# The planner's durations corrected, and two small steps given a choice of engine

## The chip, the cores and the metric

The kernel runs on one core of one Trainium2 chip. Five engines work side by side, each through its own instruction queue in order: PE (TensorE, matrix products), DVE (VectorE), ACT (ScalarE), POOL (GpSimd) and SP (SyncE, which issues the DMA transfers here). They meet through semaphores. The metric is the device time of one execution in microseconds.

## The reference

Attention with decay for 8 batches of 8 heads, 576 positions and 64 columns a head, and behind it a feed-forward layer with the Mish gate on 4608 rows:

```
scores = scale * np.matmul(q, k.transpose(0, 1, 3, 2))
cum = np.cumsum(np.log(np.clip(f, 0.0001, 1.0)), axis=-1)
decay = cum[:, :, :, None] - cum[:, :, None, :]
scores = np.where(causal, -1000000000.0, scores + decay)
attn = np.exp(scores - np.max(scores, axis=-1, keepdims=True))
attn = attn / (np.sum(attn, axis=-1, keepdims=True) + 1e-09)
x = np.matmul(attn, v)          # heads side by side: 4608 x 512
h = x @ w_in                    # 512 x 2048
sp = np.where(h > 20.0, h, np.log1p(np.exp(np.minimum(h, 20.0))))
out = (h * np.tanh(sp)) @ w_out # 2048 x 512
```

## The kernel before

**The work.** Heads go in pairs: 4 pairs a batch, 32 pairs in all. For the first 6 pairs the row maxima are found in a pass of their own (`max_items`): scores on PE, maxima on DVE (tiles `mx`, `m`), a transpose on PE and a copy of the turned maxima into the tile `mr`, from where DMAs put them beside the scores' operands. The other 26 pairs find maxima and exponentials in one pass (`new_st_items`; DVE writes `mn`, ACT the exponentials into `st`), split them in two halves of 16 bits (`hb`) and turn them by DMA (`pt`). The products with the values stand in a PSUM bank as four or five blocks of 128 rows by 65 columns; the 65th column is the row's sum. DVE turns the sums into factors (`rr`), and the division is the product of each block with its factor, from the bank into the tile `x`. `x` is split in two halves (`xp`) and turned by DMA into `xa`, the feed-forward layer's operand. That layer works in 9 chunks of 512 rows (8 of the batches, the ninth of what the batches leave over) and 16 steps of 128 hidden columns: products of `xa` with the weights `wall`, Mish on ACT (`me`), two halves for the next product (`gh`, `gl` on DVE, some `gh` on ACT), and products of those with the second weights. Products of the layer are 3456 of 512 columns.

**Tables on ACT.** Mish and the exponential lie in different function tables, so ACT loads a table each time that it goes from one to the other.

**Banks.** Of PSUM's eight banks four hold the layer's sums, two its hidden values; after the opening all of attention shares the two that are left.

**Order.** Nothing of the order is written by hand. Class `Program` records every operation, its reads and writes, and runs a model of the five queues (`schedule`): forward, always taking the ripe operation with the lowest rank, then backward to get ranks from the end, ten forward passes in all; the order of the best forward pass is issued. `choose` records an operation that may run in several ways, each on one engine, and the forward pass takes the way that ends sooner in the model. `cost` gives the model's duration of one operation. Two constants, `TSWAP` and 1370 ns, are the model's price for a table. In the opening, until the first product with `wall`, the forward pass also puts in products of the identity with itself where the model has PE idle: filler products, 128x128, which nobody reads (line 307 of before, 311 of the changed kernel). All other operations are issued from one line (310 of before, 314 of the changed kernel), so tiles tell them apart in the profile, not lines.

**Lines the change touches.** The division in `one` of `pv_items` and `new_pv_items` is one DVE instruction over all blocks; in `new_pv_items` the fifth block is one `tensor_scalar` more. The copy into `mr` in `fin` is a DVE copy. In `cost` a `tensor_scalar` between buffers in SBUF is reckoned at 1.92 elements a ns, whatever the strides, and only `scalar_tensor_tensor` is charged 60 ns for a scalar that comes from memory.

Of the kernel before, what the change touches and what calls it, by code (L numbers as in the profile page):

```python
# [13 lines left out]
F16 = mybir.dt.float16  # L14
# [6 lines left out]
AF = mybir.ActivationFunctionType  # L21
ALU = mybir.AluOpType
# [4 lines left out]
P = 128  # L27
S = 576
D = 64
# [119 lines left out]
class Program:  # L149
# [24 lines left out]
    def choose(self, *ways):  # L174

        r, w, opts = [], [], []
        for way in ways:
            total, port = 0.0, False
            for nth, (eng, method, a, kw) in enumerate(way):
                aps = [(k, x) for k, x in list(enumerate(a)) + list(kw.items()) if hasattr(x, "tensor")]  # L180
                w += [z for k, x in aps if k in ("out", "accum_out", 0) for z in self.region(x)]
                r += [z for k, x in aps if k not in ("out", "accum_out", 0) for z in self.region(x)]
                if eng == "scalar":
                    (r if method == "activation" else w).append(("table", 0, 1, 0, 1))
                if eng == "tensor":

                    out = kw["out"] if "out" in kw else a[0]
                    w.append((out.tensor.name + "/pe", 0, 1, 0, 1))
                port |= self.shared(eng, method, aps)
                cost = self.cost(eng, method, kw, aps)  # L190
                if isinstance(cost, tuple) and total:

                    total = (
                        total[0] + (53 if nth == 1 else 8 if nth % 2 else cost[0]), total[1] + cost[1], 0, cost[3])
                else:
                    total = cost if isinstance(cost, tuple) else total + cost + (80 if total else 0)
            opts.append((eng, way, total, port))
        key = len(self.ops)
        if self.rank is not None:
            key, self.rank[1] = self.rank[0] + self.rank[1], self.rank[1] + self.rank[2]  # L200
        self.ops.append((opts, r, w, key))
        self.floors.append(self.floor)
        func = ways[0][0][3].get("func") if ways[0][0][0] == "scalar" and len(ways) == 1 else None
        self.sets.append("mish" if func == AF.Mish else "exp" if func == AF.Exp else None)

        self.banks.append({
            x.tensor.name for _, _, a, kw in ways[0] for x in list(a) + list(kw.values())
            if hasattr(x, "tensor") and x.space == PSUM})
# [26 lines left out]
    def cost(self, eng, method, kw, aps):  # L235

        out = next((x for k, x in aps if k in ("out", 0)), None)
        srcs = [x for k, x in aps if k in ("in_", "in0", "in1", "data0")]
        n = max([free(x) for x in srcs[:1]] + [1]) if method == "tensor_reduce" else free(out) if out is not None else 1
        psum = any(x.space == PSUM for x in srcs)  # L240
        if method.startswith("dma_start"):
            size = free(out) * int(out.shape[0]) * mybir.dt.size(out.dtype)
            if method == "dma_start_transpose":
                return 1190 + size / 3000.0 + DH, size / 292.0
            return (450 if DRAM in (kw["in_"].space, out.space) else 625) + DH, size / DRATE
        if eng == "tensor":

            rows = int(kw.get("in_", kw.get("rhs")).shape[0])
            half = (int(out.offset) // int(out.ap[0][0]) // 64 + 1) * (int(out.shape[0]) == 64)
            part = rows * (free(kw["lhsT"]) if "lhsT" in kw else int(out.shape[0])) / 128.0**2  # L250
            if kw.get("rhs") is not None and kw["rhs"].dtype == F32:
                part *= 4 * n
                n = max(4 * n, 4 * int(out.shape[0]) + 22)
            else:
                part *= n
            return max(n, 64), part, half, int(out.shape[0]) == 64
        if eng == "scalar":
            if method != "activation":
                return 1283
            t = (51 if psum else 93) + n / 1.2  # L260
            t += 93 * any(k in ("scale", "bias") for k, x in aps) + 93 * ("accum_out" in kw)
            return t
        if eng == "vector":
            if method == "reciprocal":
                return 68 + 6 * n
            fast = method in ("tensor_scalar", "tensor_copy") and not psum
            if method == "tensor_tensor_reduce":
                return 76 + n / 0.96 + 60 * hasattr(kw["scalar"], "tensor")
            return 68 + n / (1.92 if fast else 0.96) + 60 * (method == "scalar_tensor_tensor" and "scalar" in dict(aps))
        if method == "tensor_tensor":  # L270
            b = kw["in1"]
            return 148 + (1.88 if mybir.dt.size(b.dtype) == 2 and int(b.ap[-1][0]) == 1 else 2.1) * n
        if method == "tensor_scalar":
            return 247 + 0.83 * n
        if method == "affine_select":
            return 136 + 0.85 * n
        return 43 + 0.82 * n
# [97 lines left out]
    def forward(self, deps, succ, rank):  # L375
        ops = self.ops
        n = len(ops)
# [11 lines left out]
        table = "exp"  # L389

        left, half, mode, recent = {}, 0, False, []

        def arrive(i):
            for o, (q, _, _, _) in enumerate(ops[i][0]):
# [24 lines left out]
        while len(order) < n + fills:  # L419
            clock["sync"] = max(clock["sync"], hw, dma - BACK)  # L420
            best = None
            for q in self.NAMES:
# [5 lines left out]
                if r or c:  # L428
                    t = clock[q] if r else max(clock[q], c[0][0])
                    if best is None or (t, q) < best:  # L430
                        best = (t, q)
            t, q = best
            while coming[q] and coming[q][0][0] <= t:
                _, i, o = heappop(coming[q])
# [59 lines left out]
            else:  # L494
                if q == "tensor":
                    filling = filling and ops[i][0][o][1][0][3].get("lhsT", self.idle[1]).tensor.name != self.last
                    e, full = clock[q], t - IDLE
                    while recent and recent[0][0] < t - TICK:
                        recent.pop(0)
                    dense = sum(w for _, w in recent)  # L500
                    while filling and began and e < full and dense < NEED:
                        k = int((e + 197.0) / TICK)
                        warm = left.get(int(e / TICK) - 1, 0.0) >= WARM
                        e += P / (2.4 if warm else 1.2) + 2.5
                        left[k] = left.get(k, 0.0) + P
                        recent.append((e, P))
                        dense += P * (e >= t - TICK)
                        order.insert(-1, (-1, 0))
                        fills += 1
                    began = True  # L510
                    t = max(t, e)
                    cols, weight, h, m = cost
                    if m != mode:
                        t += 97.0
                    mode = m
                    slow = 1.0 if left.get(int(t / TICK) - 1, 0.0) >= WARM else 2.0
                    cost = 22.0 if h and half and h != half else cols * slow / 2.4 + (2.5 if slow < 2 else 0.0)
                    a, b = (t + 197.0) / TICK, (t + 197.0 + cols * slow / 2.4) / TICK
                    for k in range(int(a), int(b) + 1):
                        left[k] = left.get(k, 0.0) + weight * (min(b, k + 1) - max(a, k)) / (b - a)  # L520
                    half = h
                    recent.append((t + cols * slow / 2.4, weight))
                elif lock:
                    port = max(t, port) + cost
                    cost = port - t
                elif q == "scalar" and self.sets[i] not in (None, table):
                    table = self.sets[i]
                    cost += 1370.0
                clock[q] = t + cost
# [70 lines left out]
def attn_moe(ctx: ExitStack, tc: tile.TileContext, qk, v, f, w_in, w_out, out):  # L600
# [423 lines left out]
    def max_items(g):  # L1024
# [63 lines left out]
        def fin():  # L1088
# [5 lines left out]
            ps = bank(f"mtp{g}", (P, P), F16)  # L1094
            nc.tensor.transpose(out=ps[0:9, :], in_=m16, identity=idh)
            mr = sp.tile([9, P], F16, name=f"mr{g}", tag="mr", bufs=2)
            nc.vector.tensor_copy(out=mr, in_=ps[0:9, :])
            for j in range(2):
                nc.sync.dma_start(
                    out=q1[MROW : MROW + 1, j, 0:CH].rearrange("o (t c) -> o t c", c=P),  # L1100
# [184 lines left out]
    def new_pv_items(g):  # L1285
# [29 lines left out]
        def one(j):  # L1315
# [17 lines left out]
            nc.vector.reciprocal(out=rr, in_=rr)  # L1333
            if j == 0:
                s["x"] = sp.tile([P, 10, D], F32, name=f"x{g}", tag="x32", bufs=NX)
            nc.vector.tensor_tensor(
                out=s["x"][:, j:8:2], in0=o[:, 0:4, 0:D],
                in1=rr[:, 0:4].unsqueeze(2).to_broadcast([P, 4, D]), op=ALU.mult)
            if j:
                nc.vector.tensor_scalar(  # L1340
                    out=s["x"][:, 8:10], in0=o[:, 4:5, 0:D].to_broadcast([P, 2, D]),
# [4 lines left out]
    def pv_items(g):  # L1346
# [30 lines left out]
        def one(j):  # L1377
# [5 lines left out]
            nc.vector.reciprocal(out=rr, in_=rr)  # L1383
            if j == 0:
                s["x"] = sp.tile([P, 10, D], F32, name=f"x{g}", tag="x32", bufs=NX)
            nc.vector.tensor_tensor(
                out=s["x"][:, j::2], in0=o[:, :, 0:D],
                in1=rr.unsqueeze(2).to_broadcast([P, 5, D]), op=ALU.mult)

        return [(lambda: one(0), 45 * 30), (lambda: one(1), 40 * 30)]  # L1390

# [335 lines left out]
```

## Time and profile before

| | |
|---|---|
| median of 3 runs | 1024.47 us (1024.3 to 1038.92) |
| the profiled execution, its own time | 1024.42 us |
| its span, first to last instruction | 1022.6 us |
| instructions | 19788 |
| PE busy | 986.9 us |
| DVE busy | 698.1 us |
| ACT busy | 690.9 us |

Outside the span lie 1.8 us. Busy times are sums over the span; consecutive instructions of one engine overlap a little in the records, and a PE that is busy is not PE at its peak.

### The profile page before, as it was taken

To read this page: it belongs to the slowest core of one execution; us is meant where nothing else is said; L and a number is where in the kernel's file an instruction comes from. 1 tells how busy PE (TensorE), PEld (TensorE's weight loads), DVE (VectorE), ACT (ScalarE), POOL (GpSimd) and SP (SyncE) were. 2 spreads that over 40 slices of the span, in tenths; PEclk is the share of its full clock that TensorE was granted. 3 is DMA by queue.
4 is the path that set the end of the run, shared out by engine and by line. 5 is a ranking of instruction groups with operands and counts; after the bars stand their busy time and mean duration, and the time that the engine had idled before them with its cause. 6 is when DMAs were issued, how large, how long until landed. Compare 5 with 4: busy or idle time off the path is not lost.

```text
span 1022.6 us, 19788 instructions
## 1 busy us (share of the span) xinstructions
PE 986.9 (97%) x7296; PEld 524.1 (51%) x7296; DVE 698.1 (68%) x1960; ACT 690.9 (68%) x1236; POOL 9.3 (1%) x56
## 2 busy tenths in 40 slices
PE   4999999989999999999999999999999999999998
PEld 3886564444554555554445555554555554444443
DVE  8999999977877877787777877787776562121211
ACT  6766989868778877787777786787777763212112
POOL 1000000000000000000000000000000000000000
PEclk9999999999999999999999999999999999999999
DMA  7889577987776876678777677767666431001001
GB/s 233 277 227 280 193 189 164 225 188 165 152 151 152 189 156 136 143 174 154 139 138 176 144 165 138 159 135 132 117 138 108 78 68 55 1 1 42 1 0 42
DMA packets 251644, 141.25 MB, mean 138 GB/s; under 512 B 220172, under 2 KB 220556, under 8 KB 251546
## 3 DMA queue, kind: packets, MB, share of 16 engines
q1 hardware_dynamic: 251546, 139.98, 60.4%
q8 instruction: 57, 0.93, 0.4%
q14 instruction: 41, 0.34, 0.1%
HBM read 47.76 MB, written 11.76 MB: 58 GB/s over the span
## 4 chain that ended last, share of the span: by engine, by line
PE 67%; DVE 10%; ACT 9%; DMA 7%; issue 3%; SPq 1%; ACTq 0%; DVEq 0%
PE b L310 66%; DMA st<-hl 3%; DMA qk<-in_qk_dram 2%; ACT L310 2%; ACT st L310 2%; DVE wall L310 2%; DVE hl L310 2%; DMA pt<-hb 2%; DVE b L310 1%; ACT junk L310 1%; DVE hb L310 1%; ACT me L310 1%; ACT hb L310 1%; SPq L310 1%; DVE gl L310 1%
## 5 line engine op out<-in xcount | busy, mean ns | idle before, releaser
L310 PEld LDWEIGHTS <-wall 128*128 128x128 f16 x3456 | 330.2, 98 | 373.4 <-issue 4.3
L310 PE MATMUL b<-xa,wall 128*128 128x512 f16 x1728 | 402.9, 379 | 2.8 <-ACT me L310 2.5
L310 PE MATMUL b<-gh,wall 128*128 128x512 f16 x1152 | 360.0, 379 | 0.6 <-DVE ot L310 0.6
L310 PE MATMUL b<-gl,wall 128*128 128x512 f16 x576 | 218.3, 379 | 0.0
L310 ACT ACTIVATE me<-b,cinv 128x512 f32<-128x512 f32 x144 | 93.0, 684 | 123.3 <-PE b L310 122.7
L310 ACT ACTIVATE st<-b,mn 128x512 f32<-128x512 f32 (+2 forms) x260 | 125.0, 523 | 66.6 <-DVE mn L310 50.5
L310 PE MATMUL b<-st 70*128 70x128 f16 (+15 forms) x948 | 142.2, 288 | 23.4 <-DVE qt L310 13.7
L310 DVE TENSOR_TENSOR hb<-st,hb 128x512 f16<-128x512 f32 x156 | 107.2, 688 | 67.8 <-ACT hb L310 67.1
L310 DVE TENSOR_SCALAR gh<-me,gsc 128x512 f16<-128x512 f32 x117 | 54.3, 481 | 140.1 <-ACT me L310 139.0
L310 ACT ACT_TABLE_LOAD x110 | 141.1, 1283 | 1.9
L310 PE MATMUL b<-vv,pt 128*128 128x65 f16 (+5 forms) x2520 | 116.8, 204 | 4.4 <-DMA pt<-hb 2.2
L310 PEld LDWEIGHTS <-st 70*128 70x128 f16 (+4 forms) x948 | 72.5, 103 | 80.3 <-issue 27.5
L310 DVE CUSTOM_DVE_ANT_0 b<-b,mskw 128x512 f32<-128x512 f32 (+1 forms) x208 | 102.2, 497 | 16.6 <-PE b L310 10.8
L310 ACT ACTIVATE hb<-st 128x512 f16<-128x512 f32 x156 | 97.2, 629 | 20.0 <-DMA pt<-hb 19.0
L310 DVE SCALAR_TENSOR_TENSOR gl<-me,gsc,gh 128x512 f16<-128x512 f32 x144 | 102.3, 746 | 0.6
L310 PEld LDWEIGHTS <-pt 128*128 128x128 f16 (+1 forms) x2184 | 70.0, 101 | 25.3 <-DMA pt<-hb 4.9
L310 DVE SCALAR_TENSOR_TENSOR hl<-qk,qt,hl 128x576 f16<-128x576 f32 x64 | 50.9, 811 | 3.3 <-ACT hl L310 3.1
L310 ACT ACTIVATE junk<-qk 128x576 bf16<-128x576 f32 x64 | 43.6, 682 | 9.8 <-DMA qk<-in_qk_dram 8.9
L310 DVE SCALAR_TENSOR_TENSOR wall<-wall 128x512 int32<-128x512 int32 x64 | 42.8, 676 | 0.1
L310 PEld LDWEIGHTS b<-vv,pt 128*128 128x128 f32 (+1 forms) x336 | 38.4, 184 | 3.5 <-issue 1.0
L310 ACT ACTIVATE ot<-b,cols 128x512 f32<-128x512 f32 x36 | 23.9, 684 | 21.5 <-PE b L310 12.1
L310 ACT ACTIVATE vv<-v,cols 128x576 f16<-128x576 f32 (+1 forms) x21 | 16.2, 772 | 31.5 <-PE b L310 31.5
(107 smaller groups left out, 646.1 us busy)
## 6 DMA issues: line engine op xcount, KB each, us to landing
st<-hl SPq DMA_DIRECT2D x186, 144.0 KB
qk<-in_qk_dram SPq DMA_DIRECT2D x32, 576.0 KB
v<-in_v_dram SPq DMA_DIRECT2D x32, 288.0 KB
out_dram<-ot SPq DMA_DIRECT2D x36, 256.0 KB
wall<-in_w_in_dram SPq DMA_DIRECT2D x16, 512.0 KB
wall<-in_w_out_dram SPq DMA_DIRECT2D x16, 512.0 KB
pt<-hb SPq DMA_TRANSPOSE x156
part<-ot SPq DMA_DIRECT2D x8, 256.0 KB
```

Source lines behind the costliest of these rows:

```text
L310: r = getattr(real[eng], method)(*a, **kw)
```

## The change

Three things. The division and the copy into `mr` may now run on DVE or on ACT, as the model chooses; on ACT the division is one ACTIVATE for each block of 64 columns, with the factor as its scale. `cost` charges 60 ns for any scalar from memory (`gh`, `hl`, the fifth block's `x`), takes the fast rate only where the input's and output's strides make one run (the copy of values into `vv` has gaps of one column), and 110 ns more for ACT's copies to 64 partitions of 16 bits. The forward pass charges 175 ns (DVE) or 126 ns (ACT) for a reduction right behind another one, and 8 ns instead of 80 between the parts of a way on ACT.

```
-                    total = cost if isinstance(cost, tuple) else total + cost + (80 if total else 0)
+                    total = cost if isinstance(cost, tuple) else total + cost + ((8 if eng == "scalar" else 80) if total else 0)
...
+            if int(out.shape[0]) == 64 and kw["in_"].dtype == F16:
+                t += 110
...
-            fast = method in ("tensor_scalar", "tensor_copy") and not psum
+            dims = [(int(s), int(m)) for s, m in list(out.ap)[1:] if m > 1]
+            whole = all(a == b * m for (a, _), (b, m) in zip(dims, dims[1:]))
+            fast = method in ("tensor_scalar", "tensor_copy") and not psum and whole
...
-            return 68 + n / (1.92 if fast else 0.96) + 60 * (method == "scalar_tensor_tensor" and "scalar" in dict(aps))
+            return 68 + n / (1.92 if fast else 0.96) + 60 * ("scalar" in dict(aps) or "scalar1" in dict(aps))
...
+        summed = dict(vector=[175.0, False], scalar=[126.0, False])
...
-                elif q == "scalar" and self.sets[i] not in (None, table):
+                if q in summed:
+                    sums = "accum_out" in way[0][3]
+                    cost += summed[q][0] * (sums and summed[q][1])
+                    summed[q][1] = sums
+                if q == "scalar" and self.sets[i] not in (None, table):
...
-            nc.vector.tensor_copy(out=mr, in_=ps[0:9, :])
+            nc.choose(*(scaled(mr, ps[0:9, :], None, e) for e in ("vector", "scalar")))
...
-            nc.vector.tensor_tensor(
-                out=s["x"][:, j::2], in0=o[:, :, 0:D],
-                in1=rr.unsqueeze(2).to_broadcast([P, 5, D]), op=ALU.mult)
+            nc.choose(
+                [("vector", "tensor_tensor", (), dict(
+                    out=s["x"][:, j::2], in0=o[:, :, 0:D],
+                    in1=rr.unsqueeze(2).to_broadcast([P, 5, D]), op=ALU.mult))],
+                [("scalar", "activation", (), dict(
+                        out=s["x"][:, 2 * t + j], in_=o[:, t, 0:D], func=AF.Copy, scale=rr[:, t : t + 1]))
+                    for t in range(5)])
```

The other division, in `new_pv_items`, is changed alike with four blocks. Since ranks and choices all hang on the model, every engine's order is another one. Counted over the built programs: of 64 divisions 24 go to ACT (5 of the first twelve, which have five blocks, and 19 of four blocks, 101 ACTIVATEs in all), and all 6 copies into `mr`. From DVE to ACT go also 8 of the 32 copies into `vv`, 6 of the 64 into `hl` and 3 of the 144 into `gh`; from ACT to DVE 15 of the 32 wide copies into `xp` and 2 of the 32 into `wall`. ACT loads 112 tables in place of 110 and PE has 178 filler products in place of 120. All other instructions are the same in number and engine.

Three places. First the DVE queue in the opening, where the first pair is divided, of before. Names are a tile's, with its buffer's number; `b_0_...` are PSUM banks.

```order
L310 TENSOR_SCALAR rr_146<-b_0_122 128x5
L310 TENSOR_SCALAR wsq<-wsq 128x6
L310 SCALAR_TENSOR_TENSOR wall<-wall 128x512
L310 RECIPROCAL rr_146<-rr_146 128x5
L310 TENSOR_REDUCE mx_144<-b_0_123 128x4
L310 TENSOR_TENSOR x_0_147<-b_0_122,rr_146 128x5x64
```

The same place of the DVE queue now:

```order
L314 TENSOR_SCALAR rr_146<-b_0_122 128x5
L314 TENSOR_SCALAR wall<-wall 128x512
L314 RECIPROCAL rr_146<-rr_146 128x5
L314 TENSOR_REDUCE mx_144<-b_0_123 128x4
L314 SCALAR_TENSOR_TENSOR wall<-wall 128x512 x3
L314 TENSOR_SCALAR wall<-wall 128x512
L314 SCALAR_TENSOR_TENSOR wall<-wall 128x512
```

And the ACT queue at that place now:

```order
L314 ACTIVATE mr_138<-b_0_125 9x128
L314 ACTIVATE junk_107,wsq<-wall 128x512
L314 ACTIVATE x_0_147<-b_0_122,rr_146 128x64 x5
L314 ACTIVATE junk_107,vc_155<-v_4_142 128x576
L314 ACTIVATE junk_107,vc_155<-v_5_143 128x576
L314 ACTIVATE junk_107,wsq<-wall 128x512
```

The division of the first half left DVE for ACT as five instructions, and DVE fills the place with the conversion of weights.

Second the PE queue some fifty rows in, between the maxima of the first pair (`st_0`) and of the second (`st_1`), of before:

```order
L310 MATMUL b_0_125<-st_0_81 64x64
L310 LDWEIGHTS idm
L310 MATMUL b_0_125<-msk_77,idm 128x64
L310 LDWEIGHTS st_1_82
L310 MATMUL b_0_121<-st_1_82 128x128
```

And now:

```order
L314 MATMUL b_0_125<-st_0_81 64x64
L314 LDWEIGHTS idm
L314 MATMUL b_0_125<-msk_77,idm 128x64
L311 LDWEIGHTS idh
L311 MATMUL b_0_105<-idh 128x128
L311 LDWEIGHTS idh
L311 MATMUL b_0_105<-idh 128x128
L311 LDWEIGHTS idh
L311 MATMUL b_0_105<-idh 128x128
L311 LDWEIGHTS idh
L311 MATMUL b_0_105<-idh 128x128
L314 LDWEIGHTS st_1_82
```

Four filler products came in ahead of the second pair; 54 more are spread over the rest of the opening. Ahead of the first product with `wall` stand 505 other products in before and 518 now.

Third the ACT queue in the middle of the program, where one pair has its exponentials between two loads for Mish, of before:

```order
L310 ACT_TABLE_LOAD
L310 ACTIVATE st_2_83<-b_0_125,mn_178 128x512
L310 ACTIVATE hb_181<-st_2_83 128x512
L310 ACTIVATE hl_111<-qk_0_103,qt_108 128x576
L310 ACTIVATE st_2_83<-b_0_119,mn_178 128x512
L310 ACTIVATE hb_182<-st_2_83 128x512
L310 ACTIVATE st_2_83<-b_0_125,mn_178 128x128
```

And now:

```order
L314 ACT_TABLE_LOAD
L314 ACTIVATE st_2_83<-b_0_125,mn_178 128x512
L314 ACTIVATE hb_181<-st_2_83 128x512
L314 ACTIVATE hl_111<-qk_0_103,qt_108 128x576 x2
L314 ACTIVATE vv_141<-v_1_113,cols 128x9x64
L314 ACTIVATE st_2_83<-b_0_119,mn_178 128x512
L314 ACTIVATE x_0_147<-b_0_125,rr_159 128x64 x4
L314 ACTIVATE st_2_83<-b_0_125,mn_178 128x128
L314 ACTIVATE hb_182<-st_2_83 128x512
```

Between the exponentials of one pair ACT now also has a copy of values, one `hl` more and the division of an earlier pair.

## Rows read from the trace of the kernel before

**Rows 1.** The page: busy us of the span, and tenths by slice.

```profile
PE 986.9 (97%) x7296; PEld 524.1 (51%) x7296; DVE 698.1 (68%) x1960; ACT 690.9 (68%) x1236; POOL 9.3 (1%) x56
...
PE   4999999989999999999999999999999999999998
...
PEclk9999999999999999999999999999999999999999
```

**Rows 2.** Busy us of each engine in four stretches; POOL, clock, DMA behind.

```profile
0.00:100.00 100.00, 83.63 (x800) 66.30 (x801) 92.42 (x258) 68.07 (x143) 5.51 (x29) 1.00 0.87 252
100.00:250.00 150.00, 142.28 (x1001) 76.39 (x1000) 134.33 (x403) 128.65 (x247) 0.84 (x6) 1.00 0.77 192
250.00:845.00 595.00, 587.87 (x4698) 303.11 (x4697) 439.90 (x1252) 453.13 (x785) 2.90 (x21) 1.00 0.69 141
845.00:1022.60 177.60, 173.10 (x802) 78.27 (x800) 31.44 (x50) 41.09 (x63) 0.00 (x0) 1.00 0.06 20
```

**Rows 3.** What PE waited for: us in total, times, longest.

```profile
PE b L310 <- DVE qt L310: 13.7, 1, 13.7
PE b L310 <- ACT st L310: 5.8, 8, 1.2
PE b L310 <- ACT me L310: 2.5, 2, 1.4
...
PE b L310 <- DVE x L310: 1.7, 2, 1.3
```

**Rows 4.** Groups of DVE by form: busy us, mean ns, then idle before.

```profile
L310 DVE TENSOR_SCALAR gh<-me,gsc 128x512 f16<-128x512 f32 x117 | 54.3, 481 | 140.1 <-ACT me L310 139.0
...
L310 DVE SCALAR_TENSOR_TENSOR wall<-wall 128x512 int32<-128x512 int32 x64 | 42.8, 676 | 0.1
...
L310 DVE TENSOR_TENSOR x<-b,rr 128x256 f32<-128x256 f32 x52 | 21.9, 421 | 3.7 <-ACT st L310 3.3
...
L310 DVE TENSOR_SCALAR hl<-qk,qt 128x576 f16<-128x576 f32 x34 | 17.4, 517 | 15.2 <-DMA st<-hl 14.7
...
L310 DVE TENSOR_SCALAR vv<-v,cols 128x576 f16<-128x576 f32 x10 | 8.0, 803 | 0.0
...
L310 DVE TENSOR_TENSOR x<-b,rr 128x320 f32<-128x320 f32 x12 | 5.8, 481 | 0.0
...
L310 DVE CAST xp<-x 128x512 f16<-128x512 f32 x7 | 2.9, 418 | 0.0
...
L310 DVE COPY mr<-b 9x128 f16<-9x128 f16 x6 | 1.2, 208 | 0.2 <-PE b L310 0.2
```

**Rows 5.** Groups of ACT by form: busy us, mean ns, then idle before.

```profile
L310 ACT ACT_TABLE_LOAD x110 | 141.1, 1283 | 1.9
...
L310 ACT ACTIVATE pt<-b 128x512 f32<-128x512 f32 x36 | 20.0, 592 | 3.8 <-PE b L310 3.6
...
L310 ACT ACTIVATE xp<-x 128x512 f16<-128x512 f32 x25 | 15.6, 624 | 4.4 <-DVE x L310 4.4
L310 ACT ACTIVATE vv<-v,cols 128x576 f16<-128x576 f32 x16 | 12.4, 772 | 29.5 <-PE b L310 29.5
...
L310 ACT ACTIVATE e<-b 128x64 f32<-128x64 f32 x6 | 1.3, 222 | 4.6 <-PE b L310 4.5
```

**Rows 6.** Timeline of ACT at 288 us: start, us, what.

```profile
288.01 0.35 ACT L310 ACTIVATE st<-b,mn 128x128 f32<-128x128 f32 x1
288.37 1.28 ACT L310 ACT_TABLE_LOAD   x1
289.67 1.26 ACT L310 ACTIVATE me<-b,cinv 128x512 f32<-128x512 f32 x2
```

**Rows 7.** Timeline of PE: filler products at either clock, start, us, what.

```profile
19.52 1.70 PE L307 MATMUL b<-idh 128*128 128x128 f16 x14
...
83.01 2.40 PE L307 MATMUL b<-idh 128*128 128x128 f16 x40
```

**Rows 8.** Products with `wall`: duration ns min/median/max, first and last start us.

```profile
L310 PE MATMUL b<-xa,wall x1728: 376/379/390, 90.6 to 1007.4; 128*128 128x512 f16 x192
```

More of the change, by code (lines that the diff above doesn't have):

```diff
@@ L1335, in one @@
                 s["x"] = sp.tile([P, 10, D], F32, name=f"x{g}", tag="x32", bufs=NX)
-            nc.vector.tensor_tensor(
-                out=s["x"][:, j:8:2], in0=o[:, 0:4, 0:D],
-                in1=rr[:, 0:4].unsqueeze(2).to_broadcast([P, 4, D]), op=ALU.mult)
+            nc.choose(
+                [("vector", "tensor_tensor", (), dict(
+                    out=s["x"][:, j:8:2], in0=o[:, 0:4, 0:D],
+                    in1=rr[:, 0:4].unsqueeze(2).to_broadcast([P, 4, D]), op=ALU.mult))],
+                [("scalar", "activation", (), dict(
+                        out=s["x"][:, 2 * t + j], in_=o[:, t, 0:D], func=AF.Copy, scale=rr[:, t : t + 1]))
+                    for t in range(4)])
             if j:
@@ L1385, in one @@
                 s["x"] = sp.tile([P, 10, D], F32, name=f"x{g}", tag="x32", bufs=NX)
-            nc.vector.tensor_tensor(
-                out=s["x"][:, j::2], in0=o[:, :, 0:D],
-                in1=rr.unsqueeze(2).to_broadcast([P, 5, D]), op=ALU.mult)
+            nc.choose(
+                [("vector", "tensor_tensor", (), dict(
+                    out=s["x"][:, j::2], in0=o[:, :, 0:D],
+                    in1=rr.unsqueeze(2).to_broadcast([P, 5, D]), op=ALU.mult))],
+                [("scalar", "activation", (), dict(
+                        out=s["x"][:, 2 * t + j], in_=o[:, t, 0:D], func=AF.Copy, scale=rr[:, t : t + 1]))
+                    for t in range(5)])
         return [(lambda: one(0), 45 * 30), (lambda: one(1), 40 * 30)]
```

## The prediction

> **What bounds the kernel now.** Start with the page's busy times and slices [rows 1]: PE is busy for 986.9 of 1022.6 us, near nine tenths in every slice but the first, at a granted clock near full throughout, while DVE and ACT stand at 68%. So the question is not how fast DVE or ACT are, but how much time PE loses, and where. The split in four stretches answers the second half [rows 2]. In the first 100 us PE loses 16.4, from 100 to 250 us 7.7, from 250 to 845 us 7.1, and from 845 us to the end 4.5: 35.7 in all. The last stretch holds the feed-forward layer alone (DVE 31 and ACT 41 of 178 us), and its loss is the drain of the last outputs. PE's own waits say the same from the other side [rows 3]: the longest is the first, 13.7 us until the first operands are ready, and the longest after it is 1.3 us. What the change can touch is therefore 35.7 - 13.7 - 4.5 = 17.5 us of idle time, in many small pieces. To that come filler products in the opening, 120 of them; they are busy time that does no work.
>
> One step further: where is an engine other than PE near its limit? From 100 to 250 us DVE is busy 134.3 of 150 and ACT 128.7, because weights are still converted there beside attention; in the opening DVE has 92.4 of 100 [rows 2]. After 250 us they fall to 74% and 76%. So DVE's and ACT's work is worth time before 250 us; behind that only the order is.
>
> **What leaves DVE and what comes to ACT.** DVE loses 19 x 0.421 + 5 x 0.481 = 10.4 us of division, 6 x 0.208 = 1.2 of `mr`, 8 x 0.803 = 6.4 of `vv`, 6 x 0.517 = 3.1 of `hl` and 3 x 0.481 = 1.4 of `gh`; it gains 15 x 0.418 = 6.3 of `xp` and, by `gh`'s row, 2 x 0.481 = 1.0 of `wall` [rows 4]. Sum: 15 us less, 683 for 698.
>
> The division on ACT is not in the trace, an ACTIVATE of 64 columns from PSUM with a scale from memory. The nearest row is the one without that scale, `e`, 0.222 us [rows 5]. A scale from memory adds 0.1: the pair of `me` (512 columns from PSUM, with such a scale) takes 1.26 us, and one of `pt` (the same without) 0.592, so a pair of `me` without overlap would be above 1.18 [rows 5, 6]. Bounds for one: 0.2 if consecutive ones overlap as that pair does by about a tenth, 0.32 if not. I take 0.21, since they stand back to back: 101 x 0.21 = 21 us (32 at the other end). The copy of `mr` costs 6 x about 0.27, by `e`'s row and its 64 columns more: 1.6. Then 17 copies of `vv`, `hl` and `gh` at up to 0.772 are 13, 17 fewer of `xp` and `wall` by `xp`'s row, 0.624, are 10.6, and two more tables 2 x 1.283 = 2.6 [rows 5]. Sum: 27 us more (38 at most), 718 for 691. Neither engine reaches PE's load; on the whole this costs nothing, hidden behind PE's products.
>
> On the tables: in the trace a load is followed by the next ACTIVATE at once (288.37 + 1.28, next start 289.67), and the ACTIVATE ahead ends where the load starts [rows 6], so I price a switch at its load. The Trainium skill ("ScalarE: Activation LUTs", What ACT_TABLE_LOAD costs) adds about 1380 ns of drain to the 1283 ns of a load; the load agrees with the row, the drain is not to be seen in it, and by the page the two tables would cost 5.3 us on ACT in place of 2.6.
>
> **The opening.** The first product with `wall` starts at 90.6 us [rows 8]; it needs the fourth pair's `x`, split and turned. I counted what stands on DVE ahead of the fourth pair's split: 223 instructions before, 225 now. Four divisions, five `mr` and two scalings of weights are gone (1.9 + 1.0 and, at `wall`'s 0.676 each, 1.4 us); but 5 conversions of `wall` (5 x 0.676 = 3.4), 3 `hl` (1.6), an `xp` (0.4) came in, and four maxima and two shorter steps of conversion, taken at half of 0.676 each (2.0) [rows 4]. Net 3 us more ahead of that point. The conversions are not new, only earlier: up to the 17th `gl` DVE has 2.5 us less to do than before, ACT up to the 17th `me` 6 us more. PE's opening grows by 3 us less the thirteen products that now come ahead of `wall`, about 1 us. The 58 further fillers are priced from both ends. If they lie in waits that PE has anyway, they cost nothing; the four ahead of the second pair do, where PE now waits for maxima. If all push, they cost 58 x 0.06 = 3.5 us at the spacing of 83 us (40 in 2.40) or 58 x 0.12 = 7 at that of 19.5 us (14 in 1.70), which is half the pace [rows 7]. I take nothing: the model puts them where it sees PE idle, and DVE's 3 us make such a place. Opening: +2 us (0 to +7; not under 0, since DVE's queue there is longer).
>
> **100 to 250 us.** DVE, the fuller engine, is 2.5 us ahead of before at the 17th `gl`, having been 3 behind at the start; ACT is 6 behind and has 21 us of air in this stretch [rows 2]. Half of DVE's gain on PE's 7.7 us of idle seems fair, and the truer durations help most where engines are full: -2 us (-6 to +5, where +5 is ACT's 6 us more, if it becomes the late one).
>
> **250 to 845 us.** The old table was short by 60 ns for each of 117 `gh`, 34 `hl` and 26 of the fifth block's `x`, and for `vv` reckoned 0.37 us where the row has 0.803: in all some 14 us that DVE was later than planned [rows 4]. PE's order follows the plan, so a truer plan makes it ask less often for what is not there. But PE idles for 7.1 us only, and what it names is mostly ACT's `st`, 5.8 over the whole run [rows 2, 3], the engine that now gets more. -2 us (-6 to +8: everything gone, or the moved divisions felt).
>
> **The sum.** Against the profiled execution's 1024.4 us: +2 - 2 - 2 gives 1022.4, and the median of the runs is the same within 0.1. I predict 1022 us. Two per cent, about what a measurement of this kernel can tell from no change, is 1004 to 1045.
>
> **Rivals.** *The truer plan takes nearly all waits away.* PE's waits between start and drain fall from 17.5 to about 5, and the opening doesn't grow: 1024.4 - 12 = 1012. For it: PE's waits are short and many, as a misjudged order makes them. Against: the opening's queue is longer by count, and a constant such as `TSWAP` was left as it stood. Even all 17.5 us give 1007, so a gain of over 2% needs a shorter opening on top.
>
> *The divisions on ACT hold PE up.* A division frees its PSUM bank. On DVE it took 0.42 to 0.48 us, on ACT four or five times 0.21 and one more semaphore from `rr`, so 0.5 to 0.7 us longer; and it stands in a queue where two tables and a pair of Mish, 1.28 x 2 + 1.26 = 3.8 us, can be ahead of it [rows 5, 6]. Attention has two banks; PE's next scores wait for one. If each of the 24 divisions is felt by its own length, that is 24 x 0.6 = 14 us, and with a third of the queue ahead 24 x 1.2 more, so 1037 to 1066. I put it at 1037 to 1045. It decides if PE's waits name `x` on ACT for over 10 us. For it: ACT's waits of `st` already head PE's list. Against: the plan charges these holds, and PE has products with `wall` to put between. The Trainium skill ("ScalarE: Activation LUTs", Rules for kernel authors) speaks on this side: it gives multiplications to VectorE and not to ScalarE. By length alone the row of DVE, 0.421 for all blocks, agrees with it; what the page leaves open is which engine has time.
>
> *The order is just another draw.* Nothing systematic comes of it, the small waits fall elsewhere: 1024 +- 5. This isn't told apart from the forecast by the time alone.
>
> **How the numbers follow.** Forecast with the last rival, 1015 to 1031: 0.64. Nearly all waits gone, 1007 to 1015: 0.16, of it under 1004 no more than 0.02. ACT holds PE up, 1031 and more: 0.20, of it over 1045 0.07. The range of 8 in 10 takes the forecast's whole, most of the first rival and half of the second: 1010 to 1036. The terms' ends, -12 and +20, would reach 1012 to 1044; all three late at once is unlikely. Chances: 0.02 faster, 0.91 within 2%, 0.07 slower.
>
> **What the profile after would show.** PE still near 987 us busy plus up to 4 of fillers; the first product with `wall` at 92 to 94 us; DVE near 683 and ACT near 718; an ACTIVATE of `x` of 0.3 us in the records, four in about 0.95; attention's end still near 845 us, and the last stretch as before. PE's waits from 100 to 845 us should fall from 14.8 to about 11. I am wrong if the opening lengthens by much more than DVE's 3 us (then the fillers push, or `mr` on ACT comes late), or if PE waits for ACT's `x`.

## The result and the profile after

The changed kernel takes 1013.82 us (median), the kernel before 1024.24 in the same runs: a ratio of 0.9909, 95% interval 0.9896 to 0.9922. That is 10 us less, against a forecast of 2 less. Some executions of any of these kernels run their opening at a lower granted clock and are longer for it; the comparison leaves the most disturbed ones out, and where it matters below a time stands with its execution's mean granted clock.

The page of the changed kernel, to be read against [rows 1]:

```profile
span 1011.2 us, 19990 instructions
...
PE 985.7 (97%) x7354; PEld 526.0 (52%) x7354; DVE 688.0 (68%) x1930; ACT 713.9 (71%) x1345; POOL 9.3 (1%) x56
```

PE's busy time is what it was, within 1.2 us, with 58 filler products more in it. DVE has 10 us less and ACT 23 more. Nearly the whole gain is idle time of PE: 25.5 us in place of 35.7, 10.2 of the 11.4 us by which the span is shorter. The four stretches of [rows 2], of the changed kernel:

```profile
0.00:100.00 100.00, 84.03 (x866) 69.07 (x867) 91.94 (x264) 73.16 (x176) 5.51 (x29) 1.00 0.89 247
100.00:250.00 150.00, 146.05 (x1041) 78.68 (x1040) 138.27 (x403) 134.12 (x257) 0.84 (x6) 0.99 0.81 200
250.00:845.00 595.00, 593.30 (x4700) 304.86 (x4699) 429.30 (x1221) 468.97 (x857) 2.91 (x21) 1.00 0.68 140
845.00:1011.20 166.20, 162.29 (x752) 73.40 (x750) 28.51 (x45) 37.69 (x57) 0.00 (x0) 0.99 0.05 19
```

In the second stretch PE idles for 4.0 us in place of 7.7, in the third for 1.7 in place of 7.1; in the first and the last it idles as before (16.0 and 3.9 us for 16.4 and 4.5). The last split of `x` starts at 833.1 us in place of 843.9, so attention ends 11 us earlier and the gain lies ahead of its end. DVE and ACT are both busier in the second stretch than before: that stretch got denser on all three engines. What PE waits for between 100 and 845 us, of the changed kernel (us, times, longest):

```profile
PE b L314 <- DVE wsc L314: 1.5, 2, 1.3
PE b L314 <- DMA pt<-hb: 1.3, 2, 0.8
PE b L314 <- DVE x L314: 0.7, 1, 0.7
...
PE b L314 <- ACT st L314: 0.3, 1, 0.3
```

ACT's `st`, first on the list in [rows 3] with 5.8 us behind the start, is down to 0.3. ACT's new work and DVE's division, of the changed kernel by form:

```profile
L314 ACT ACT_TABLE_LOAD x112 | 143.7, 1283 | 2.1
L314 ACT ACTIVATE x<-b,rr 128x64 f32<-128x64 f32 x101 | 23.2, 318 | 2.5 <-DVE rr L314 1.6 <-DVE top L314 0.8
L314 ACT ACTIVATE mr<-b 9x128 f16<-9x128 f16 x6 | 1.6, 262 | 4.3 <-PE b L314 4.3
```

```profile
L314 DVE TENSOR_TENSOR x<-b,rr 128x256 f32<-128x256 f32 x33 | 13.9, 420 | 1.3 <-ACT st L314 0.9
L314 DVE TENSOR_SCALAR x<-b,rr 128x128 f32<-128x128 f32 x26 | 9.0, 348 | 12.9 <-ACT x L314 12.5 <-ACT st L314 0.4
```

The products with `wall`, against [rows 8]:

```profile
L314 PE MATMUL b<-xa,wall x1728: 376/379/634, 92.5 to 996.6; 128*128 128x512 f16 x192
```

They start 1.9 us later and end 10.8 earlier: 904.1 us from the first to the last in place of 916.8. This length leaves the opening out, but not what a lower clock costs just behind it, and I use it below as a measure beside the time. Each length is from one profiled execution.

### The profile page after: what moved, and what is told of

Same layout as the page of the kernel before. It is cut to its first block, busy times and chain, and to the rows that moved or that the text cites. A ratio compares the mean times of both kernels' runs of the same rounds, so it can differ in the third digit from the quotient of the medians.

```text
span 1011.2 us, 19990 instructions
## 1 busy us (share of the span) xinstructions
PE 985.7 (97%) x7354; PEld 526.0 (52%) x7354; DVE 688.0 (68%) x1930; ACT 713.9 (71%) x1345; POOL 9.3 (1%) x56
## 4 chain that ended last, share of the span: by engine, by line
PE 76%; ACT 8%; DVE 7%; DMA 6%; issue 2%; SPq 1%; ACTq 0%; DVEq 0%
PE b L314 75%; DMA st<-hl 3%; ACT L314 2%; DMA pt<-hb 1%; DVE b L314 1%; ACT junk L314 1%; ACT st L314 1%; PE b L311 1%; ACT me L314 1%; DVE wall L314 1%; DVE hl L314 1%; DVE hb L314 1%; ACT hb L314 1%; SPq L314 1%; DVE st L314 1%
## 5 line engine op out<-in xcount | busy, mean ns | idle before, releaser
L314 PE MATMUL b<-st 70*128 70x512 f16 (+16 forms) x948 | 140.3, 286 | 17.0 <-DVE qt L314 13.4
L314 ACT ACTIVATE st<-b,mn 128x512 f32<-128x512 f32 (+2 forms) x260 | 127.1, 525 | 41.5 <-DVE mn L314 19.6
L314 PEld LDWEIGHTS <-st 70*128 70x128 f16 (+5 forms) x948 | 70.9, 102 | 70.1 <-issue 15.8
L314 ACT ACTIVATE vv<-v,cols 128x576 f16<-128x576 f32 (+1 forms) x29 | 22.2, 770 | 45.6 <-PE b L314 45.6
L314 ACT ACTIVATE ot<-b,cols 128x512 f32<-128x512 f32 x36 | 23.9, 686 | 21.5 <-PE b L314 10.9
```

The source lines that it names most:

```text
L314: r = getattr(real[eng], method)(*a, **kw)
```

## The experiments

Three theories. **A**: the corrected durations make the order fit what the engines deliver. **B**: the division that left DVE pays, in the stretch where DVE is full. **C**: a new order is a draw, and this one was lucky. Each kernel was timed in three rounds beside the kernel before. Times of before in the three batches were 1023.36, 1023.61 and 1023.49 us.

### The durations alone, the choices alone

`costs_only` is the changed kernel with the division and the copy into `mr` on DVE as before:

```
-            nc.choose(*(scaled(mr, ps[0:9, :], None, e) for e in ("vector", "scalar")))
+            nc.vector.tensor_copy(out=mr, in_=ps[0:9, :])
```

(the two divisions likewise). 

> The model's corrected durations as in the changed kernel, but division and turned maxima stay on DVE. Theory A (the truer plan makes PE's order fit what the other engines deliver): most of the 10 us is here, 1013 to 1017 us, PE's idle time from 100 to 845 us falls from 14.8 to below 8. Theory B (moving the division off DVE is what pays, where DVE is full from 100 to 250 us): at most 3 us are here, 1021 to 1024. Theory C (any new order is a draw): anything from 1012 to 1030.

`choices_only` is the kernel before with the three `choose` calls of the changed kernel and the old durations. 

> Division and turned maxima may go to ACT, the model's durations are the old ones. Theory A: 1021 to 1026 us, PE's waits as before. Theory B: 1013 to 1017 us. Theory C: anything from 1012 to 1030.

Measured: durations alone 0.9946 (0.9917 to 0.9975), median 1018.75; at granted clocks of 0.998 and more 1013.8, 1015.5, 1016.1 and 1020.4, below that 1016.9 to 1024.6. PE's idle time from 100 to 845 us is 7.6 us, below the 8 of theory A. Choices alone 1.0106 (1.0021 to 1.0191): the one execution at clock 1.000 took 1027.7, three at 0.98 took 1042 to 1044.6. With the old durations the choice of engine gained nothing, and lost 4 us in that one execution. But few divisions moved to ACT in it, 9 (37 ACTIVATEs) in place of 24 (101):

```profile
L310 ACT ACTIVATE x<-b,rr 128x64 f32<-128x64 f32 x37 | 8.5, 315 | 0.1
```

So this run says little of 24 divisions on ACT, and B falls by `costs_only`: with none of them there, and 1016.5 us on average at 0.998 and more, the durations carry some 7 of the 10 us.

### The same model, another order

`before_nz` and `after_nz` put noise on the first pass's ranks:

```
-NZ = 0
+NZ = 40
```

> The kernel before with noise of up to 40 places on the first pass's ranks: nothing but another order of the same model, with the old durations. Theories A and B: 1021 to 1028 us, the model's error stays. Theory C: it may well be 1014 or 1034; a change of over 5 us either way says that one order tells little.

> The changed kernel with the same noise on the first pass's ranks. Theories A and B: 1011 to 1018 us, since durations and choices are the same. Theory C: back towards 1022 or above.

Measured: `before_nz` 1.0046 (1.003 to 1.0063), `after_nz` 1.0008 (0.9972 to 1.0045); at clock 1.000 the latter took 1019.0 to 1021.6. In both the first score product now waits until 17.7 us for a DMA, 4 us later than the first product in the kernels without noise. So the noise went into the opening, which I had not wanted, and the runs were made again with noise behind the opening alone:

```
-        rank = [x[3] + NZ * float(draw.random()) for x in self.ops]
+        rank = [x[3] + NZ * float(draw.random()) * (i > 1400) for i, x in enumerate(self.ops)]
```

> The kernel before with noise of up to 40 places on the first pass's ranks, but only behind the opening, so that the opening's first operands come as early as before. Theory A: 1020 to 1026 us, since the durations are the old ones. Theory C: a change of over 5 us either way at the same granted clock.

> The changed kernel with the same noise behind the opening alone. Theory A: 1011 to 1017 us. Theory C: it loses half or more of the 10 us.

Measured: `before_late` 1.0057 (1.003 to 1.0085), 1025.7 to 1029.9 at 0.996 and more; `after_late` 0.9997 (0.9972 to 1.0023), 1018.4 to 1021.5 at 0.998 and more. By the expectations both noisy forms of the changed kernel fall to C: they lie above A's ranges and lose more than half of the 10 us. `before_nz`, 5 us longer, falls to C narrowly, and `before_late`, 4 us longer, lies between. So C is right in part: with this noise either model is 4 to 7 us behind its order without noise, and a good share of a difference of 10 us can be order alone. All four moves go to the slower side, and all come of one seed, so it isn't shown whether the orders without noise were lucky or noise as such costs this. A holds beside it, by a comparison that I made afterwards: in each of the three pairs the corrected model is 8 to 10 us ahead of the old one under the same noise (1024 to 1014 without, 1029 to 1020 with noise everywhere, 1028 to 1020 with noise behind the opening, at clocks of 0.996 and more).

### Which of the corrections

`sums_only` is the kernel before with only the charge for a reduction behind another; `rates_only` has only the 60 ns and the rate for gaps:

```
+            dims = [(int(s), int(m)) for s, m in list(out.ap)[1:] if m > 1]
+            whole = all(a == b * m for (a, _), (b, m) in zip(dims, dims[1:]))
-            fast = method in ("tensor_scalar", "tensor_copy") and not psum
+            fast = method in ("tensor_scalar", "tensor_copy") and not psum and whole
...
-  60 * (method == "scalar_tensor_tensor" and "scalar" in dict(aps))
+  60 * ("scalar" in dict(aps) or "scalar1" in dict(aps))
```

> The kernel before with one correction of the model alone: a reduction right behind another costs 175 ns (DVE) or 126 ns (ACT) more. 260 minima on DVE and 128 sums of squares on ACT are such reductions, the largest error of the old durations. Theory A (truer durations): the larger part of the corrected durations' 9 us at an undisturbed clock is here, 1014 to 1018 us. Theory C (a draw): anything from 1012 to 1030.

> The kernel before with the other corrections on DVE alone: 60 ns for a scalar from memory and the slow rate where strides leave gaps. Together some 14 us of DVE's work by the trace. Theory A: 2 to 5 us are here, 1018 to 1022 us. Theory C: anything from 1012 to 1030.

What the charge for a reduction stands for can be read on DVE in the kernel before: behind the read of a minimum's accumulator (`mn`) another operation often starts at once, and another minimum 0.17 us later.

```profile
302.87 0.14 DVE L310 DVE_READ_ACCUMULATOR2_ANT mn<- 128x1 f32 x1
302.87 0.42 DVE L310 TENSOR_TENSOR x<-b,rr 128x256 f32<-128x256 f32 x1
...
310.66 0.14 DVE L310 DVE_READ_ACCUMULATOR2_ANT mn<- 128x1 f32 x1
310.83 0.76 DVE L310 CUSTOM_DVE_ANT_0 b<-b,mskw,mn 128x512 f32<-128x512 f32 x1
```

But of the 260 minima only 95 follow another one directly in that trace (start to start 0.175 us in the median), and of the 128 sums on ACT 49 (0.219 us, with another operation behind 0.093). So the charge is some 17 us of DVE and 6 of ACT, and not 260 and 128 times its amount.

`after_nosums` and `after_norates` take one of the two out of the changed kernel:

```
-        summed = dict(vector=[175.0, False], scalar=[126.0, False])
+        summed = dict(vector=[0.0, False], scalar=[0.0, False])
```

> The changed kernel with the charge for reductions that follow each other set to zero; the other corrections and the choices stay. Read at a granted clock of 0.996 and more, and by the time from the first to the last product of xa with wall, which leaves the opening out: 904 us in the changed kernel, 917 in the kernel before. Theory A, with the sums as the main error: 1018 to 1024 us and 912 to 918 from first to last. If the other corrections carry it: 1012 to 1016 and 904 to 910.

> The changed kernel with DVE's old rates (no 60 ns for a scalar from memory, the fast rate for gaps); the sums' charge and the choices stay. If the sums carry the gain: 1012 to 1016 us at an undisturbed clock, 904 to 910 from the first to the last product with wall. If the rates do: 1018 to 1024 and 912 to 918.

Measured: `sums_only` 1.015 (1.011 to 1.019), its four executions at clocks of 0.97 to 0.989 and so no measure of the order; `rates_only` 1.0022 (0.9995 to 1.005), 1020.6 to 1022.9 at 0.997 and more; `after_nosums` 1.0029 (1.0 to 1.0058), 1020.7 at clock 1.000; `after_norates` 1.0031 (1.0012 to 1.0049), 1023.8 at 1.000. Theory A expected `sums_only` at 1014 to 1018 us at an undisturbed clock, which none of its executions had; by the length below it gains nothing. Neither half alone gives what the whole gives, and taking either out of the changed kernel loses it, at clock 1.000 in one execution each. Each of the last two came where it was expected if the half taken out carries the gain, which both can't do alone. By time alone a draw of 5 us could do that, and the choices are made anew in each kernel, too: 31 divisions are on ACT without the sums' charge and 29 without the new rates, 24 in the changed kernel. The stretch from 100 to 250 us tells more. Its row in the kernel without the sums' charge, and in the one without the new rates:

```profile
100.00:250.00 150.00, 139.09 (x997) 75.63 (x994) 133.90 (x399) 130.86 (x258) 1.01 (x6) 1.00 0.81 206
```

```profile
100.00:250.00 150.00, 140.25 (x986) 75.17 (x986) 134.74 (x397) 128.72 (x251) 1.27 (x6) 0.99 0.75 192
```

PE idles there for 10.9 and 9.8 us, in the changed kernel for 4.0. (The first of the two rows is from an execution at a mean clock of 0.988, whose first product with `wall` came at 100.0 us, so its stretch holds earlier work.) Over all profiled kernels, two of which are told further down (PE's idle us from 100 to 250 us and from 100 to 845 us; us from the first to the last product of `xa` with `wall`):

| kernel | idle 100 to 250 | idle 100 to 845 | first to last |
|---|---|---|---|
| before | 7.7 | 14.9 | 916.8 |
| rates_only | 6.8 | 11.5 | 915.3 |
| sums_only | 7.4 | 14.4 | 917.9 |
| choices_only | 7.9 | 15.6 | 921.3 |
| before_nz | 8.4 | 12.3 | 916.2 |
| before_late | 5.0 | 15.2 | 919.4 |
| after_nosums | 10.9 | 16.4 | 917.1 |
| after_norates | 9.8 | 15.3 | 917.5 |
| **costs_only** | 4.2 | 7.6 | 910.4 |
| **costs_late** | 4.3 | 8.6 | 911.5 |
| **after_nz** | 2.1 | 9.0 | 910.0 |
| **after_late** | 2.5 | 8.6 | 911.5 |
| **after_nofill** | 5.3 | 8.0 | 904.7 |
| **after** | 4.0 | 5.7 | 904.1 |

The first column crosses (`before_late` and `after_nofill`), the two others do not. By length the six kernels that have all corrections (bold) lie at 904 to 912, the eight that lack any at 915 to 921. By PE's idle time from 100 to 845 us they lie at 5.7 to 9.0 and at 11.5 to 16.4. No draw crosses either gap, though by length draws differ by 7 among themselves, more than the gap's 4. The lower clock behind the opening is in some of the lengths, most in `costs_only` (clock 0.78 here) and `costs_late` (0.77 from 98.8 to 120 us):

```profile
95.10:120.00 24.90, 22.36 (x107) 9.86 (x106) 22.82 (x58) 19.69 (x41) 0.00 (x0) 0.78 0.62 191
```

That can be up to 5.5 us of the first's 910.4 and 4.9 of the second's 911.5 (the share of full speed that was not granted, times the stretch). With this taken off everywhere the two groups lie at 902 to 910 and at 913 to 921.

ACT's `st` isn't what the corrections mend as such: PE still waits for it for 3.3 us in `costs_only`, 4.7 in `after_late` and 5.3 in `after_nz`, so the 0.3 belongs to the one order of the changed kernel.

### What the choices add

`costs_late` is `costs_only` with the noise of `after_late`, for a second pair. 

> Corrected durations, division and turned maxima on DVE, with the noise behind the opening that after_late has. A second pair for what the choices are worth. Theory A: within 3 us of after_late at an undisturbed clock (1018 to 1022), 908 to 914 from first to last, so the choices add little. Theory B: 4 or more above it.

Measured 0.9989 (0.9968 to 1.0011), 1016.5 and 1020.2 at 0.998: beside `after_late`'s 1018.4 to 1021.5 no difference. In the first pair the changed kernel is at 1011.7 to 1015.2 where `costs_only` is at 1013.8 to 1020.4, clocks of 0.998 and more. So the choices are worth nothing in one order and 2 or 3 us in the other, as far as the four executions of `costs_only` tell, which are 7 us apart; the medians' further distance (1018.75 to 1013.82) goes with `costs_only`'s clocks, which were below 0.998 in six of ten executions.

### The fillers

`after_nofill` has no filler products:

```
-NEED = 6200.0
+NEED = 0.0
```

> The changed kernel without filler products in the opening. If they only take waits that PE has anyway and nothing hangs on them: 1008 to 1014 us, the granted clock as before. If the clock falls where PE waits: the granted clock of the stretch from 40 to 100 us near 0.5, the first product with wall later than 100 us, 1025 to 1050.

Measured 0.9995 (0.9965 to 1.0025), median 1021.34; 1030.8 twice and 1052.3 stand at clock 1.000 too, so the mean clock doesn't account for these three. Neither expectation came whole: the granted clock is as before, but the first product with `wall` comes after 100 us, and the time lies between the two ranges. The products with `wall`, of this kernel:

```profile
L314 PE MATMUL b<-xa,wall x1728: 376/379/391, 100.7 to 1005.4; 128*128 128x512 f16 x192
```

They start 8.2 us later than in the changed kernel and then take 904.7 us for 904.1: the gain of that length does not hang on the fillers. The timeline of PE without fillers at 54 us (start, us, what):

```profile
54.20 0.31 PE L314 MATMUL b<-idm,msk 128*128 128x128 f16 x1
...
54.74 0.31 PE L314 MATMUL b<-idm,msk 128*128 128x128 f16 x1
```

and with them, in the changed kernel, at 20 us:

```profile
19.68 0.31 PE L314 MATMUL b<-msk,idm 128*128 128x128 f16 x1
19.79 2.12 PE L311 MATMUL b<-idh 128*128 128x128 f16 x18
...
22.13 1.46 PE L311 MATMUL b<-idh 128*128 128x128 f16 x17
...
23.49 0.22 PE L314 MATMUL b<-msk,idm 128*128 128x128 f16 x1
```

A product of 128 columns takes 0.31 us in one and 0.22 at the end of the other; these are the two paces that the spacing in [rows 7] shows, 0.12 us a product at 19.5 us and 0.06 at 83. The title of [rows 7] speaks of either clock, but the granted clock of both places reads 1.00 in the profile, so the spacing alone shows them. Without fillers PE works at the slower pace until 58.5 us at least; in the changed kernel it is at the faster one at 23.5 us, behind runs of 18 and 17 fillers. In before, with fewer fillers, that comes later:

```profile
25.98 1.91 PE L307 MATMUL b<-idh 128*128 128x128 f16 x16
...
29.50 0.31 PE L310 MATMUL b<-idm,msk 128*128 128x128 f16 x1
...
29.82 0.22 PE L310 MATMUL b<-idm,msk 128*128 128x128 f16 x1
```

## Why the prediction was right, and where it was small

**Right.** PE's time bounds the kernel, DVE's and ACT's busy time costs nothing as such: 23 us more on ACT came with 10 us less in all. The prices held: the division on ACT is 0.318 us in the records (0.3 forecast), four of them in a row take 0.92 us (0.95 forecast), 23.2 us in all for 21. DVE came to 688 us for 683 and ACT to 714 for 718, a change of 10 less and 23 more where 15 and 27 were summed. The first product with `wall` came at 92.5 us, in the forecast 92 to 94. That the 58 further fillers would push nothing fits PE's busy time, which fell by 1.2 us with them in it: the faster pace came 6 us earlier than in before. That the opening's 1.9 us are DVE's queue alone is argued from counts and not shown.

**Too small.** The time fell inside the stated 1010 to 1036 us, but not in the forecast's own 1015 to 1031: the way was right, the size a fifth of what came, and the range held it because it took in most of the first rival, which had a chance of 0.16. "Half of DVE's gain on PE's 7.7 us of idle seems fair": -2 us was put down for the stretch from 100 to 250 us and -2 for that to 845, and PE lost 3.8 and 5.4 us less, both inside the bounds of -6. Together with 1.0 at both ends that is the 10.2 us of idle time; the rest of the span's 11.4 is 1.2 us of busy time. The opening's +2 was there at the first product with `wall` and not in the end: by the 193rd the changed kernel is level (207.9 us for 208.5), so this term is to be read with the next one and not by itself. That conversions done earlier made up for it is argued from the counts and not shown. From there on it draws ahead, and with that attention's end, forecast near 845 us, came at 833. The term most mis-sized is the one from 250 to 845 us. It was held down because ACT, the engine that PE named there, was to get more work; ACT got 16 us more in that stretch, and PE waited less. One reading was off: the longest of PE's waits behind the first is 1.4 us in [rows 3] and not 1.3, which changes nothing.

**The rivals.** The first, nearly all waits gone and 1012 us, is nearest to what came. PE's idle time between start and drain (25.5 us less the first wait of 13.4 and the last stretch's 3.9) fell from 17.5 to 8.2 us and not to 5, and the time is 1013.8. Its mechanism is shown as far as the runs go: with all corrections PE idles less in every order tried, without either half it doesn't. That ACT's divisions hold PE up did not come: PE names `x` on ACT nowhere. The wait went to DVE, whose fifth block's `x` now idles 12.5 us behind ACT's `x`, 15 times, where PE hardly feels it (it waits once for DVE's `x`, 0.7 us). The Trainium skill's rule that gives multiplications to VectorE ("ScalarE: Activation LUTs", Rules for kernel authors) agrees with the trace by length, 0.42 us for four blocks on DVE and 0.92 on ACT. For the kernel's time it decided little: the choices, with 20 and 24 divisions on ACT in the two pairs, were worth 0 to 3 us. "Just another draw" was undervalued: it is no rival at all to the others but works beside them, with the 4 to 7 us that the noise cost.

**Still open.** Which single correction mends which wait can't be read from these runs: the halves don't add up (from the first to the last product 1.5 us less with the rates alone and 1.1 more with the sums alone, 6 less with all of the durations and 13 with the choices on top; up to 5.5 us of the step from 6 to 13 can be `costs_only`'s lower clock). The two small corrections on ACT (110 ns, 8 for 80) were not tried alone, and the second prices the division there: 9 divisions went to ACT under the old durations and 24 under the new.

## What to carry to other kernels

Where a planner fixes the order, put its durations to the start-to-start spacing of the trace before tuning anything else, and all at once: half of the corrections gave little or nothing here, and a new choice of engine under wrong durations gained nothing. Before a gain of half a per cent is put down to an idea, run the same program in another order of the same model: here that alone moved the time by as much. And read the gain from a length that leaves out a noisy part of the program, not from the median alone, and look at the clock in what is left.

## What the runs showed of the hardware that I had not expected

The granted clock of the opening can decide more than the change: 14 to 17 us between executions of one kernel, against 10. In the kernel with the choices alone (stretches of the opening; the third number from the end is the granted clock):

```profile
20.00:40.00 20.00, 18.05 (x182) 14.84 (x179) 18.77 (x56) 13.21 (x30) 0.20 (x2) 1.00 0.83 252
40.00:60.00 20.00, 18.77 (x148) 16.46 (x147) 14.78 (x39) 13.65 (x35) 0.11 (x1) 0.78 0.88 224
60.00:80.00 20.00, 20.00 (x114) 15.56 (x113) 11.17 (x33) 9.57 (x20) 0.11 (x1) 0.50 0.64 183
80.00:100.00 20.00, 20.00 (x167) 17.32 (x167) 12.28 (x35) 9.31 (x21) 0.11 (x1) 0.69 0.43 110
```

the same stretches of the changed kernel:

```profile
20.00:40.00 20.00, 19.75 (x224) 17.24 (x222) 18.50 (x56) 14.05 (x38) 0.20 (x2) 1.00 0.90 274
40.00:60.00 20.00, 19.75 (x209) 16.07 (x209) 18.95 (x54) 16.70 (x46) 0.23 (x2) 1.00 0.93 224
60.00:80.00 20.00, 19.61 (x224) 16.75 (x221) 18.20 (x49) 13.47 (x33) 0.11 (x1) 1.00 0.91 245
80.00:100.00 20.00, 19.54 (x177) 15.03 (x176) 18.71 (x69) 15.99 (x40) 0.11 (x1) 1.00 0.97 257
```

PE waits in the first for 1.3 and 1.2 us between 20 and 60 us, the clock goes to 0.50 (1.2 of 2.4 GHz), and from 60 to 80 us PE is wholly busy with half as many products (114 for 224), while DVE is busy for 11 of the 20 us in place of 18: at that clock PE is the opening's bound. That execution took 1044.6 us, one of the same kernel at clock 1.000 1027.7. The fall comes in some executions of a kernel and not in others, and `sums_only`, `after_nosums` and `choices_only` (99 to 114 fillers) have it more than the changed kernel (178). But `after_late` with 194 had it too, once at 0.975, and the kernel before with 120 only once in each batch of 19, 25 and 27 (0.992, 0.981 and 0.964), so the count of fillers alone does not explain it. The granted clock of a stretch is also no full account of the pace at the start: without fillers the row of the first 100 us gives 1.00 although a product of 128 columns still takes 0.31 us at 54 us.
